# The first megabyte of keys in three strided transfers instead of one

## The chip, the core and the metric

The kernel runs on one core of a Trainium2 chip. The metric is the device time of one execution in microseconds. Three timed executions before the change gave 192.98, 193.03 and 193.13; their median is 193.03.

## The reference

Decode step of a gated mix of two branches: attention over a cached window and a small MLP. In short:

```
x: 8 x 1 x 448                    k_cache, v_cache: 8 x 8 x 4096 x 256 (bf16)
g = sigmoid((x * gate_w).sum(-1))
q = (x @ wq) as 16 heads of 256;  k, v = the last 1024 positions, each kv head used by 2 query heads
a = softmax(q k^T / 16) v, all heads side by side, @ wo
b = gelu(layernorm(x) @ w1 + b1) @ w2 + b2
out = g * a + (1 - g) * b
```

All inputs together that must be read are 77.67 MB, nearly all of it the 1024 cached positions of keys and values: 8 batches x 8 heads x 1024 x 256 x 2 bytes is 33.6 MB for each of the two.

## The kernel before

Everything large comes through one ring of four slots in SBUF (`ring`, `RING = 4`); a slot is 128 partitions x 32 KB, 4 MB. A list, `plan`, says in which order slots are filled: keys of batch 0, the weights wq, then for each further batch its keys and the values of the batch before it, then w1, the last values, and wo. `pump()` issues the loads of the next entries as long as fewer than four slots are in use, and `done()` frees one when its reader has been issued. All these loads are issued from one queue, SP (SyncE). Two small inputs, x and gate_w, are loaded from the ACT queue (L177, L182).

The keys of one batch are 8 heads x 1024 positions x 256. Partition p of a slot holds 32 consecutive positions: p = 4 s + a, where a is the head within a group of four heads and s (0 to 31) the block of 32 positions. One half of a slot is heads 0 to 3, the other heads 4 to 7. `kv_loader` makes one transfer for each half (16 KB in each partition, 2 MB), or more where `cuts` asks for it: for batch 0 it is `(2, 2)`, four transfers of 1 MB, each with 128 rows of 8 KB:

```
nc.sync.dma_start(
    t[:, i * HS + k * n : i * HS + (k + 1) * n],
    v[:, :, k * n : (k + 1) * n],
)
```

The source `v` has the dimensions s, a and (position in the block, head dimension); the destination `t` is taken over all 128 partitions.

Transfers are numbered round robin over eight completion semaphores in the order in which they are issued, those from ACT among them. So from the ninth on, each issue first waits until the transfer eight places before it has landed. Loads that refill a slot wait for its readers, too. SP's instructions run in order, so an issue that waits holds back all later ones.

The compute side, per batch: the keys are turned so that the head dimension lies on partitions. The first block of a batch goes by a 32 x 32 transpose on DVE (L334) and copies on POOL (L342), the other fifteen by TensorE transposes into PSUM (L364) and copies on ACT (L370) or DVE (L372). Then come scores (L431), maximum (L444), exponential (L448), the turning of the weights (L455 to L485), and the product with the values (L502). At the end TensorE multiplies by w2 and wo (L636, L647), the result is copied (L658) and stored (L659).

At the start nothing computes before keys or weights are there: L334 and L364 wait for the first MB of keys of batch 0, the query matmuls (L383, L395) for wq.

Of the kernel before, what the change touches and what calls it, by code (L numbers as in the profile page):

```python
# [17 lines left out]
def kernel(  # L18
# [15 lines left out]
    nc = tc.nc  # L34
# [11 lines left out]
    QD = 4  # L46
# [20 lines left out]
    HS = NCK * Dh  # L67
    SLOT = NG * HS
    RING = 4
    TAIL = 8  # L70
    LATE = 1
    qscale = float(Dh) ** -0.5

    xf = A_x.rearrange("b s d -> (b s) d")
# [30 lines left out]
    def add(key, loader):  # L105
        index[key] = len(plan)
        plan.append(loader)
# [1 line left out]
    def slot(*key):  # L109
        return slots[index[key]]  # L110

    def kv_loader(src, b, cuts=(1, 1), inner=False):
        pieces = [
            (i, k, cuts[i])
            for i in range(NG)
            for k in range(cuts[i])
        ]
        if inner:
            pieces.sort(key=lambda x: x[1])

        def load(t):
            for i, k, m in pieces:
                v = src[b, i * QD : (i + 1) * QD, kv_base:Sk, :].rearrange(
                    "a (s c) d -> s a (c d)", c=NCK
                )
                n = HS // m
                nc.sync.dma_start(
                    t[:, i * HS + k * n : i * HS + (k + 1) * n],
                    v[:, :, k * n : (k + 1) * n],
                )  # L130

        return load

    def rows_loader(pieces):
        def load(t):
            o = 0
            for ap in pieces:
                n = ap.shape[-1]
                nc.sync.dma_start(t[:, o : o + n], ap)
                o += n  # L140

        return load
# [11 lines left out]
    def last_values(t):  # L154
        kv_loader(A_v_cache, NB - 1, (2, 2), True)(t)
        nc.sync.dma_start(slot("w12")[:, OW2 : OW2 + FB * D], w2_v)

    add(("k", 0), kv_loader(A_k_cache, 0, (2, 2)))
    add(("wq",), rows_loader(wq_r + [wq_t]))
    for b in range(1, NB):  # L160
        add(("k", b), kv_loader(A_k_cache, b))
        add(("v", b - 1), kv_loader(A_v_cache, b - 1))
    add(("w12",), rows_loader([w1_m, w1_t]))
    add(("v", NB - 1), last_values)
    cuts = [(q, 0, J8) for q in range(NQW - 2)] + [
        (NQW - 2, 0, 4),
        (NQW - 2, 4, 8),
        (NQW - 1, 0, 2),
        (NQW - 1, 2, 5),
        (NQW - 1, 5, 7),  # L170
        (NQW - 1, 7, 8),
    ]
# [439 lines left out]
    b = NB - 1  # L612
# [30 lines left out]
    nc.vector.tensor_tensor(accs[:], A1[:], b2s[:], op=ALU.add)  # L643
    narrow.insert(TAIL - LATE, (pick[:], accs[:]))
    for i, (lhsT, rhs) in enumerate(narrow):
# [44 lines left out]
```

## Time and profile before

| | |
|---|---|
| median of 3 runs | 193.03 us (192.98 to 193.13) |
| the profiled execution, its own time | 193.1 us |
| its span, first to last instruction | 191.3 us |
| read from HBM | 77.67 MB, 406 GB/s over the span |
| busy: PE, DVE, ACT, POOL | 121.7, 108.5, 92.5, 55.6 us |
| first issue of keys on SP | at 0.73 us |
| first MB of keys landed | at 5.85 us |
| last weights landed, last PE group begins | at 186.32 and 186.36 us |

Times of events are counted from the start of the span. An engine's busy time doesn't include its waits. A transfer is issued by an instruction on a queue (SPq, ACTq), whose time is the time of issuing; the data are moved by 16 DMA engines, each taking whole rows as packets, and "landed" is when the waiting instruction could see the completion. The trace has every packet's start, size and duration, but not which of the 16 engines moved it.

### The profile page before, as it was taken

To read this page: it belongs to the slowest core of one execution; us is meant where nothing else is said; L and a number is where in the kernel's file an instruction comes from. 1 tells how busy PE (TensorE), PEld (TensorE's weight loads), DVE (VectorE), ACT (ScalarE), POOL (GpSimd) and SP (SyncE) were. 2 spreads that over 40 slices of the span, in tenths; PEclk is the share of its full clock that TensorE was granted. 3 is DMA by queue.
4 is the path that set the end of the run, shared out by engine and by line. 5 is a ranking of instruction groups with operands and counts; after the bars stand their busy time and mean duration, and the time that the engine had idled before them with its cause. 6 is when DMAs were issued, how large, how long until landed. Compare 5 with 4: busy or idle time off the path is not lost.

```text
span 191.3 us, 2889 instructions
## 1 busy us (share of the span) xinstructions
PE 121.7 (64%) x1100; PEld 78.9 (41%) x1100; DVE 108.5 (57%) x247; ACT 92.5 (48%) x104; POOL 55.6 (29%) x143
## 2 busy tenths in 40 slices
PE   0777609778775387737787677558944885073553
PEld 0656205564661186316642553156514762010111
DVE  4273783844889558705871587028722895846310
ACT  2398600994892259525862595229822892000000
POOL 8570000760760067005800480039002910000000
PEclk9997885999999969997996999859998899966555
DMA  5999999999999999999999999999999999999980
GB/s 190 432 423 426 445 423 418 414 438 432 421 430 415 432 432 425 433 428 414 425 435 432 435 411 425 432 421 433 428 421 428 425 432 406 420 422 428 409 334 4
DMA packets 7417, 77.86 MB, mean 407 GB/s; under 512 B 862, under 2 KB 1388, under 8 KB 2156
## 3 DMA queue, kind: packets, MB, share of 16 engines
q1 hardware_dynamic: 7370, 77.67, 96.5%
q8 instruction: 8, 0.13, 0.3%
q14 instruction: 5, 0.04, 0.1%
q10 hardware_dynamic: 34, 0.01, 0.0%
HBM read 77.67 MB, written 0.01 MB: 406 GB/s over the span
## 4 chain that ended last, share of the span: by engine, by line
DMA 75%; PE 10%; DVE 7%; ACT 4%; issue 1%; ACTq 0%; DVEq 0%
DMA slot<-in_A_k_cache_dram 45%; DMA slot<-in_A_v_cache_dram 14%; DMA slot<-in_A_wq_dram 8%; DMA slot<-in_A_wo_dram 7%; PE ktp L364 6%; ACT kt L370 3%; DVE kt L372 2%; PE S_ps L431 2%; DVE qw L423 1%; PE A L647 1%; DVE EZ L466 1%; DVE qt L408 1%; DVE nmx L444 1%; DVE EB L455 1%; DVE sc L464 1%
## 5 line engine op out<-in xcount | busy, mean ns | idle before, releaser
L370 ACT COPY kt<-ktp 128x1024 bf16<-128x1024 bf16 x80 | 76.7, 1020 | 37.7 <-PE ktp L364 37.4
L364 PE MATMUL ktp<-ident_f,slot 128*128 128x128 f32 x480 | 72.8, 307 | 29.7 <-DMA slot<-in_A_k_cache_dram 20.1
L364 PEld LDWEIGHTS ktp<-ident_f,slot 128*128 128x128 f32 x480 | 61.1, 158 | 48.4 <-issue 22.4
L342 POOL COPY kt<-B 32x128 f32<-32x128 f32 x128 | 51.4, 402 | 97.8 <-DVE B L334 92.8
L372 DVE COPY kt<-ktp 128x1024 bf16<-128x1024 bf16 x40 | 27.5, 687 | 17.0 <-PE ktp L364 16.8
L502 PE MATMUL PO<-slot,ET 128*16 128x512 bf16 x256 | 18.8, 441 | 17.6 <-DMA slot<-in_A_v_cache_dram 17.6
L334 DVE STREAM_TRANSPOSE B<-slot 128x512 f32<-128x512 f32 x8 | 5.7, 712 | 30.9 <-DMA slot<-in_A_k_cache_dram 30.8
L448 ACT ACTIVATE E<-S_ps,nmx 128x1024 f32<-128x1024 f32 x8 | 8.9, 1115 | 28.8 <-DVE nmx L444 28.8
L431 PE MATMUL S_ps<-kt,qw 128*4 128x512 bf16 x256 | 17.9, 419 | 5.4 <-DVE qw L423 5.4
L502 PEld LDWEIGHTS <-ET 128*16 128x16 bf16 x256 | 6.9, 96 | 28.5 <-DMA slot<-in_A_v_cache_dram 13.5
L444 DVE TENSOR_REDUCE nmx<-S_ps 128x1 f32<-128x1024 f32 x8 | 9.8, 1222 | 9.9 <-PE S_ps L431 9.9
L431 PEld LDWEIGHTS <-qw 128*4 128x4 bf16 x256 | 6.7, 85 | 13.5 <-DVE qw L423 6.2
L455 DVE STREAM_TRANSPOSE EB<-E 128x1056 f32<-128x1056 f32 x8 | 10.2, 1271 | 1.3 <-ACT E L448 1.3
L528 DVE TENSOR_TENSOR oP<-Y 32x32 bf16<-32x32 f32 x32 | 9.4, 295 | 1.1
L658 ACT CAST res<-A 8x224 bf16<-8x224 f32 x1 | 0.3, 337 | 15.8 <-PE A L647 15.8
L485 DVE TENSOR_TENSOR ET<-sm,mask 128x512 bf16<-128x512 f32 x8 | 5.5, 692 | 2.2 <-PE sm L477 2.1
L515 DVE STREAM_TRANSPOSE T<-PO 128x512 f32<-128x512 f32 x8 | 5.7, 709 | 1.0 <-PE PO L502 0.9
L570 ACT ACTIVATE zb<-za 128x448 f32<-128x448 f32 x1 | 0.6, 576 | 10.7 <-DVE za L569 10.7
L477 PE MATMUL sm<-EZ,perm 128*128 128x128 bf16 x8 | 1.7, 216 | 6.3 <-DVE EZ L466 6.3
L636 PE MATMUL A<-slot,oP 128*8 128x448 bf16 x24 | 2.9, 549 | 2.5 <-DMA slot<-in_A_wo_dram 2.5
L643 DVE TENSOR_TENSOR accs<-A,b2s 128x448 f32<-128x448 f32 x1 | 0.6, 625 | 6.6 <-PE A L636 6.6
L520 DVE TENSOR_TENSOR Y<-T 64x64 f32<-64x64 f32 x16 | 4.0, 248 | 0.6
(91 smaller groups left out, 59.6 us busy)
## 6 DMA issues: line engine op xcount, KB each, us to landing
slot<-in_A_k_cache_dram SPq DMA_DIRECT2D x14, 2048.0 KB, 28.9
slot<-in_A_v_cache_dram SPq DMA_DIRECT2D x14, 2048.0 KB, 30.8
slot<-in_A_k_cache_dram SPq DMA_DIRECT2D x4, 1024.0 KB, 10.6
slot<-in_A_v_cache_dram SPq DMA_DIRECT2D x4, 1024.0 KB, 24.8
slot<-in_A_wq_dram SPq DMA_DIRECT2D x3, 1024.0 KB, 13.3
slot<-in_A_wo_dram SPq DMA_DIRECT2D x2, 896.0 KB
slot<-in_B_w_dram SPq DMA_DIRECT2D x1, 1568.0 KB, 22.4
slot<-in_B_w_dram SPq DMA_DIRECT2D x1, 1344.0 KB
```

What stands on the lines that cost most here:

```text
L334: nc.vector.transpose(B[:].rearrange("p c w s a -> p (c w s a)"), kn[:, c0 * P : (c0 + CB) * P],)
L342: nc.gpsimd.tensor_copy(words[BL * w : BL * (w + 1), :, c0 : c0 + CB, g * S8 : (g + 1) * S8, 0], B[BL * g : BL * (g + 1), :, w].rearrange( ...
L364: nc.tensor.transpose(words[:, c, :, 0], kn[:, o : o + P], ident_f[:])
L370: nc.scalar.copy(dst, src)
L372: nc.vector.tensor_copy(dst, src)
L431: nc.tensor.matmul(S_ps[BL * t : BL * t + UR, n * QN : (n + 1) * QN], lhsT=qw[:, j, b, t, rep * u : rep * u + UR], rhs=KT[u][:, t, n * CQ ...
L444: nc.vector.reduce_max(nmx[:], S_ps[:], axis=AXIS.X, negate=True)
L448: nc.scalar.activation(E[:, 0:W], S_ps[:], ACT.Exp, bias=soft.pop(b)[:], scale=1.0, accum_out=E[:, W : W + 1],)
L455: nc.vector.transpose(EB[:].rearrange("p c r -> p (c r)"), E[:])
L502: nc.tensor.matmul(PO[BL * t : BL * t + Hq], lhsT=ET[:, c].rearrange("p u a r -> p (u a r)"), rhs=vn[:, c], start=(c < QD), stop=(c >= NCK ...
L515: nc.vector.transpose(T[:], PO[:].rearrange("p u (e j) -> p u j e", j=J8))
L528: nc.vector.tensor_tensor(oP[BL * i : BL * (i + 1), :, :, b], Yv[0:BL, :, :, i], Yv[BL : 2 * BL, :, :, i], op=ALU.add,)
```

## The change

Of the four 1 MB transfers of batch 0's keys, the first is split by partitions into three: partitions 0, 4, 8, ... (head 0, 32 rows), partitions 2, 6, 10, ... (head 2, 32 rows), and the odd partitions (heads 1 and 3, 64 rows). Rows are still 8 KB each, and each lands where it did. The other three transfers of that slot and all other loads stay as they were. The two more transfers stand on the SP queue ahead of everything that followed the first one, and take two more places in the round of semaphores.

```
+    FIRST = ((0, QD), (2, QD), (1, 2))
...
-    def kv_loader(src, b, cuts=(1, 1), inner=False):
+    def kv_loader(src, b, cuts=(1, 1), inner=False, first=((0, 1),)):
...
                 n = HS // m
-                nc.sync.dma_start(
-                    t[:, i * HS + k * n : i * HS + (k + 1) * n],
-                    v[:, :, k * n : (k + 1) * n],
-                )
+                for a, step in first if (i, k) == (0, 0) else ((0, 1),):
+                    nc.sync.dma_start(
+                        t[a::step, i * HS + k * n : i * HS + (k + 1) * n],
+                        v[:, a::step, k * n : (k + 1) * n],
+                    )
...
-    add(("k", 0), kv_loader(A_k_cache, 0, (2, 2)))
+    add(("k", 0), kv_loader(A_k_cache, 0, (2, 2), first=FIRST))
```

`QD` is 4. For all other pieces the loop runs once, over all partitions, as before.

## The prediction

> **What bounds the kernel now.** I read the page from the top, first for what is never idle.
>
> ```profile
> PE   0777609778775387737787677558944885073553
> ...
> DMA  5999999999999999999999999999999999999980
> ...
> HBM read 77.67 MB, written 0.01 MB: 406 GB/s over the span
> ...
> DMA 75%; PE 10%; DVE 7%; ACT 4%; issue 1%; ACTq 0%; DVEq 0%
> ```
>
> PE, the busiest engine, has holes in nearly every slice. The DMA row has only three that are not full, the first and the last two. Three quarters of the chain that ended last are transfers. Next, the table by stages (columns: stretch and its us, five engines, PEclk, DMA share, GB/s) shows how full "9" is, and how the stream begins.
>
> ```profile
> 2.13:2.53 0.40, 0.00 (x0) 0.00 (x0) 0.34 (x2) 0.40 (x1) 0.40 (x2) 1.00 1.89 328
> 2.53:2.93 0.40, 0.00 (x0) 0.00 (x0) 0.36 (x2) 0.38 (x1) 0.40 (x2) 1.00 0.00 0
> 2.93:3.33 0.40, 0.00 (x0) 0.00 (x0) 0.14 (x2) 0.00 (x0) 0.40 (x3) 1.00 1.26 532
> ...
> 6.00:60.00 54.00, 40.16 (x338) 27.96 (x338) 35.44 (x92) 35.01 (x39) 19.27 (x48) 0.91 1.01 427
> 60.00:120.00 60.00, 39.69 (x375) 27.39 (x376) 36.27 (x76) 32.63 (x37) 19.29 (x48) 0.91 1.01 427
> 120.00:180.00 60.00, 36.19 (x343) 21.75 (x343) 33.79 (x73) 23.22 (x27) 12.85 (x32) 0.83 1.01 424
> ```
>
> A packet counts in the stretch in which it starts. All 16 DMA engines start their first key row (8 KB) between 2.13 and 2.53; nothing starts in the next 0.4 us; the second rows start from 2.93. From there the engines run without a break to 186.3 us. The same rate holds whichever engine computes, so the time is: start of the stream + 77.67 MB at the DMA engines' rate + the tail. A DMA engine that starts earlier by some time ends the kernel earlier by that time, if its share and its rate stay. The tail, in the chain of waits:
>
> ```profile
> 172.03 14.29 DMA slot<-in_A_wo_dram
> 186.32 0.04 issue
> 186.36 2.11 PE A L647 x16
> 188.47 0.37 DVE res L658
> ```
>
> It follows the last weights and moves with them. So all depends on the first three microseconds, in the timeline and in the DMA view of 1.4 to 2.6 us (40 slices of 30 ns):
>
> ```profile
> 0.73 0.59 ACTq L177 DMA_DIRECT2D x_sb<-in_A_x_dram  x1
> 0.73 2.59 SPq L127 DMA_DIRECT2D slot<-in_A_k_cache_dram  x4
> 5.88 0.71 DVE L334 STREAM_TRANSPOSE B<-slot 128x512 f32<-128x512 f32 x1 [2.81 <-DMA slot<-in_A_k_cache_dram]
> ...
> DMA  0000000001670000000000000999999999000900
> GB/s 0 0 0 0 0 0 0 0 0 60 120 60 0 0 0 0 0 0 0 0 0 0 0 0 0 819 273 819 273 273 819 273 273 273 0 0 0 273 0 0
> ```
>
> Two transfers are issued at the same 0.73 us: x_sb, 8 rows, from ACT, and the first MB of keys, 128 rows, from SP. The rows of x_sb begin at 1.68 to 1.74 (packet starts in the trace; slices 10 to 12 above), those of the keys at 2.17 to 2.52 (slices 26 to 38), mean 2.28. So 0.95 us after the issue with 8 rows, and 1.44 us with 128.
>
> **The change, part by part.**
>
> *Earlier start of the first row.* The transfer at the head of the queue shrinks from 128 rows to 32. A straight line through the two rows above gives 0.95 + 24/120 x 0.49 = 1.05 us from issue to first packet, and the spread over the engines shrinks from 0.35 us toward the 0.05 of x_sb: 0.11. Mean start 0.73 + 1.05 + 0.06 = 1.84 instead of 2.28: gain 0.44. Lower bound 0: the two rows differ in the issuing engine and in the size of a row, too, and if the delay hangs on those nothing moves. I take the line, as the only pair that the trace has.
>
> *First row's duration.* The first key rows take 0.64 to 0.95 us (mean 0.76 over the 16 packets), all later ones of 8 KB 0.31 (median of the packets), so 0.45 us more; 6 of 8 rows of x_sb took 0.04 to 0.05, the bare time of 896 bytes. If the excess comes with the 128 rows, a line gives back 0.3 of it; if it belongs to the first access to key rows, nothing. The new first rows are key rows of 8 KB, nearest to the latter: gain 0.1, bounds 0 and 0.3.
>
> *Two more transfers on SP.* The issues of L127 take 0.54 to 0.66 us whether 8 or 16 KB a row, and L187 with only 2 rows (also at a partition step) 0.53 and 0.59, so rows do not matter to SP and I price each new one like these, 0.64 with its gap (the first four start 0.63 to 0.72 apart). All later issues on SP move back by 2 x 0.64 = 1.3 us: the second MB is issued at 2.7 instead of 1.45, the four wq transfers from 4.6 instead of 3.37. What covers it is the queue. Piece one starts at 1.84 and gives each engine 2 rows: 0.66 + 0.31, drained at 2.8. Piece two, issued at 1.4, is ready at 2.4 to 2.5, and lasts 0.62 to 3.4. Piece three, issued at 2.1, with 64 rows (line: 1.18) is ready at 3.3, lasts 1.24 to 4.7; the second MB, issued at 2.7, is ready at 4.15. Each is there before the one ahead is drained, with 0.1 to 0.5 us to spare, so it costs nothing. Without that cover (first row at its bare 0.31) piece two and three come 0.1 to 0.2 late, bound 0.2. The waits of SP's later issues on older transfers shift by two places: the wq loads now wait for x_sb, for the first two key pieces and for gate_w's row, all long landed by 4.6 to 6; k(1) waits for the third piece, issued then at about 6.3 against 6.24. From k(1)'s second half on, each waits for the same transfer as before. With 3 MB and more queued (7 us) none empties the stream.
>
> *Two more boundaries on each DMA engine.* A transfer ends on each engine with a 4-byte packet of 9 ns, and the next row starts some 10 ns later; rows just behind it take 0.31 to 0.32. So 2 x 0.02 us, and I take 0.05.
>
> *Rows and bytes* stay: 128 rows of 8 KB, the same addresses, 8 rows per engine if each piece is dealt out evenly (2, 2 and 4). The consumers (L334, L364) now wait for three transfers, of which the last lands earlier than the one does now (5.85). What was idle before them stays idle, and no engine's order changes.
>
> Sum: -0.44 - 0.10 + 0 + 0.05 = -0.49 us. The profiled execution took 193.1 (span 191.3 and 1.8 around it), so 192.6; the median is 0.07 lower: **192.55**. With all bounds: -0.44 - 0.3 + 0.05 = -0.7 to +0.25 (no gain, 0.2 late, 0.05).
>
> [...]
>
> **The rivals.**
>
> *A. The start does not move enough.* The 1.44 us come from the key rows or from SP's slower issue (0.66 against 0.59 on ACT), not from the number of rows. For: the pieces stay strided in SBUF, and L187 shows that SP needs no less for few rows. Against: between end of issue and first packet lie 0.37 us for x_sb and 0.78 for the keys, and that difference is the larger part. Time 192.7 to 193.3, most likely 192.9.
>
> *B. Slower: two DMA engines meet at one place of SBUF.* The trace shows 0.31 us per 8 KB row only for transfers of all 128 partitions. In a piece of every fourth or second partition the dealing of rows to engines is another, and where two engines write into the same part of SBUF at once they would halve each other's rate. All 8 rows of the first MB: 8 x 0.31 = +2.5, less 0.5: 195.0; in half of the rows: +1.24 - 0.49, 193.8. It decides from where the mean row of the first MB takes over 0.31 + 0.88/8 = 0.42 us (0.49 to eat the gain, 0.39 to be seen). For: no row of the trace excludes it. Against: each piece reaches across all of SBUF, and engines out of step would pass each other. [...]
>
> *C. Slower: uneven dealing.* If the small pieces of 32 rows fell on 8 engines, those would have 4 rows more each: +1.24, 193.8. Against it: the 8 rows of x_sb went to 8 engines, one each, with 8 closing packets.
>
> **How the numbers follow.** 0.2% is 0.39 us, about what a measurement of this kernel can tell from no change. Forecast (192.2 to 192.64): 0.50, since the sum needs only 0.39 of its 0.49 and the second term's bound lies above. A: 0.20, the part of the lower bounds that stays within 0.39. B: 0.22, half of it near 193.8 and half up to 195. C: 0.08. So faster 0.50, same 0.20, slower 0.30. The range reaches from all gains at their bounds with a little over for the boundary price (192.2) over A and the half-rate cases near 193.8 to 194.2, and leaves out the full case of B and of C, about 0.15, and little below. The likeliest case alone: 192.2 to 192.64.
>
> **What would show it.** In the changed profile: first key packets at 1.8 to 1.9 us instead of 2.17; no pause in packet starts after 2.9; rows of 0.31 us in the first MB; the third piece landed and L334 begun at about 5.4 instead of 5.88; the last PE group at 185.9 instead of 186.36; DMA share 1.01 in between; the end 5.0 us after. Wrong: a first packet at 2.1 or later (A); packets of 0.4 to 0.6 us before 5 us (B); engines that begin the second MB more than a row apart (C); or a stretch without packets between the pieces, which would mean that SP feeds too slowly.

## The result, and the profile after

The changed kernel took 195.24 us (median of 6 runs, 194.47 to 195.57) against 193.01 for the kernel before (6 runs, 192.98 to 193.13): ratio 1.0108, 95% interval 1.009 to 1.0126. It is slower by 2.2 us, outside the range that was forecast. The profiled execution took 194.9, with a span of 193.1 against 191.3.

Lines of the page of the changed kernel, those that answer to the ones shown of before:

```profile
DMA  5999999999999999999999999999999999999970
...
HBM read 77.67 MB, written 0.01 MB: 402 GB/s over the span
...
DMA 71%; PE 11%; ACT 6%; DVE 6%; SPq 3%; issue 2%; ACTq 0%
```

The bytes are the same and the DMA row looks the same. New is SPq with 3% in the chain that ended last: issuing on SP has become part of it. The table by stages of the changed kernel (columns as in the prediction; a packet counts in the stretch in which it starts) shows where the time went:

```profile
2.20:4.00 1.80, 0.00 (x0) 0.00 (x0) 0.77 (x4) 0.70 (x1) 1.80 (x6) 1.00 0.99 337
4.00:5.00 1.00, 0.00 (x0) 0.00 (x0) 0.00 (x0) 0.00 (x0) 0.82 (x2) 1.00 0.86 287
5.00:6.50 1.50, 0.00 (x0) 0.00 (x0) 0.00 (x0) 0.00 (x0) 0.00 (x0) 1.00 0.99 306
6.50:8.00 1.50, 1.22 (x6) 1.25 (x7) 0.71 (x1) 0.10 (x1) 0.41 (x2) 1.00 0.84 317
8.00:60.00 52.00, 37.42 (x322) 25.71 (x324) 33.23 (x87) 34.77 (x39) 18.75 (x47) 0.93 1.01 425
60.00:180.00 120.00, 75.77 (x724) 49.87 (x712) 70.10 (x151) 55.61 (x64) 32.00 (x80) 0.86 1.01 425
```

The kernel before in the first stretch and in the three that differ:

```profile
2.20:4.00 1.80, 0.00 (x0) 0.00 (x0) 0.77 (x4) 0.71 (x1) 1.80 (x6) 1.00 0.98 333
4.00:5.00 1.00, 0.00 (x0) 0.00 (x0) 0.00 (x0) 0.00 (x0) 0.83 (x2) 1.00 0.96 401
5.00:6.50 1.50, 0.51 (x3) 0.54 (x4) 0.62 (x1) 0.00 (x0) 0.00 (x0) 1.00 1.01 421
6.50:8.00 1.50, 1.50 (x9) 1.50 (x8) 0.13 (x2) 0.89 (x1) 1.22 (x4) 1.00 1.02 431
```

The last column is the one to read. Up to 4 us both move the same, then the changed kernel moves 287, 306 and 317 GB/s for 4 us where the kernel before moves 401 to 431, and from 8 us on there is no difference worth the name. The packet records say it in time: the first 0.5 MB are through at 3.78 us against 3.89 before, so 0.1 earlier; 1 MB at 5.49 against 5.08, 2 MB at 8.63 against 7.47, 3 MB at 11.10 against 9.82, and 70 MB at 168.70 against 167.46. About 1.25 us are lost by 11 us and stay lost. Between 2.2 and 11 us the 16 engines stood idle for 0.57 us each on average (0.04 before), and their rows took 1.23 us more than the usual 0.31 us a row (0.49 before). The two increases, 0.53 and 0.74, make 1.27 us. So the longer rows are the larger part.

The first stretches of the changed kernel answer to the three of the prediction: there is no pause of 0.4 us any more, since in this execution the first rows took less time (0.48 us on average, 0.76 before), but the third stretch has 351 GB/s instead of 532.

```profile
2.13:2.53 0.40, 0.00 (x0) 0.00 (x0) 0.34 (x2) 0.40 (x1) 0.40 (x2) 1.00 0.91 246
2.53:2.93 0.40, 0.00 (x0) 0.00 (x0) 0.36 (x2) 0.37 (x1) 0.40 (x2) 1.00 0.87 328
2.93:3.33 0.40, 0.00 (x0) 0.00 (x0) 0.14 (x2) 0.00 (x0) 0.40 (x3) 1.00 1.03 351
```

The start itself, in the DMA view of 1.4 to 2.6 us of the changed kernel and in its timeline:

```profile
DMA  0000000005020000000000000009999090000099
GB/s 0 0 0 0 0 0 0 0 0 179 1 60 0 0 0 0 0 0 0 0 0 0 0 0 0 0 0 546 819 819 273 0 819 0 0 0 0 0 546 546
...
0.73 3.77 SPq L129 DMA_DIRECT2D slot<-in_A_k_cache_dram  x6
4.55 3.45 SPq L141 DMA_DIRECT2D slot<-in_A_wq_dram  x4
...
6.77 0.71 DVE L336 STREAM_TRANSPOSE B<-slot 128x512 f32<-128x512 f32 x1 [3.70 <-DMA slot<-in_A_k_cache_dram]
```

Key rows begin in slice 28 (2.22 us), later than the slice 26 of before. The third piece has landed at 6.77, 0.9 us later than the whole MB did. SP issues the six key transfers 0.63 us apart, as priced, but the first two wq transfers take 0.98 and 1.17 us to issue (0.63 and 0.43 before). The tail, in the chain of waits of the changed kernel, has its old length:

```profile
173.81 14.25 DMA slot<-in_A_wo_dram
188.06 0.04 issue
188.10 2.11 PE A L649 x16
190.21 0.37 DVE res L660
```

It comes 1.74 us later. That is more than the 1.25 us of the stream, in part because the DMA engines now end further apart: the 16 closing packets of the last transfer lie at 187.36 to 188.44 (mean 187.75), before at 186.00 to 186.73 (mean 186.32). Mean +1.43, last +1.71: the tail, +1.74, goes with the last. (The profiled execution was one of the quicker ones of the changed kernel, 0.3 us below its median.)

### The profile page after: what moved, and what is told of

Same layout as the page of the kernel before. It is cut to its first block, busy times and chain, and to the rows that moved or that the text cites. A ratio compares the mean times of both kernels' runs of the same rounds, so it can differ in the third digit from the quotient of the medians.

```text
span 193.1 us, 2893 instructions
## 1 busy us (share of the span) xinstructions
PE 121.6 (63%) x1100; PEld 79.0 (41%) x1100; DVE 107.7 (56%) x247; ACT 92.1 (48%) x104; POOL 55.3 (29%) x143
## 4 chain that ended last, share of the span: by engine, by line
DMA 71%; PE 11%; ACT 6%; DVE 6%; SPq 3%; issue 2%; ACTq 0%
DMA slot<-in_A_k_cache_dram 42%; DMA slot<-in_A_v_cache_dram 13%; DMA slot<-in_A_wq_dram 9%; DMA slot<-in_A_wo_dram 7%; PE ktp L366 7%; ACT kt L372 5%; PE S_ps L433 2%; SPq L129 2%; SPq L141 1%; DVE kt L374 1%; DVE qw L425 1%; PE A L649 1%; DVE qt L410 1%; DVE nmx L446 1%; DVE EZ L468 1%
## 5 line engine op out<-in xcount | busy, mean ns | idle before, releaser
L366 PE MATMUL ktp<-ident_f,slot 128*128 128x128 f32 x480 | 73.7, 310 | 31.2 <-DMA slot<-in_A_k_cache_dram 22.3
L366 PEld LDWEIGHTS ktp<-ident_f,slot 128*128 128x128 f32 x480 | 61.8, 160 | 49.8 <-issue 25.4
L504 PE MATMUL PO<-slot,ET 128*16 128x512 bf16 x256 | 18.0, 427 | 16.5 <-DMA slot<-in_A_v_cache_dram 16.5
L504 PEld LDWEIGHTS <-ET 128*16 128x16 bf16 x256 | 6.3, 94 | 27.6 <-DMA slot<-in_A_v_cache_dram 18.8
```

The source lines that it names most:

```text
L366: nc.tensor.transpose(words[:, c, :, 0], kn[:, o : o + P], ident_f[:])
L504: nc.tensor.matmul(PO[BL * t : BL * t + Hq], lhsT=ET[:, c].rearrange("p u a r -> p (u a r)"), rhs=vn[:, c], start=(c < QD), stop=(c >= NCK ...
```

## Experiments

**Partition steps, or the number of transfers.** Rival B (here theory M) had the right size, so the first four runs part it from a queue that is fed too slowly (theory Q).

```diff
 e1_columns: the first MB by columns
+    for lo, hi in ((0, 0.25), (0.25, 0.5), (0.5, 1)):   # of the 8 KB of a row
+        nc.sync.dma_start(t[:, i * HS + c0 : i * HS + c1], v[:, :, c0:c1])
```

> The first MB again in three transfers of 256, 256 and 512 KB, but cut by columns: each has all 128 partitions, with rows of 2, 2 and 4 KB. Number, bytes and order on SP are those of the changed kernel. Theory M (in a piece with a partition step, DMA engines meet at one place of SBUF and slow each other): no meeting here, so 193.0 or a little below (192.6 to 193.2), packets of 2 KB at about 0.08 us. Theory Q (the queue is fed too slowly when transfers at its head are small; the partitions do not matter): about 195, as changed, with DMA engines idle between 4 and 7 us.

195.31 us, ratio 1.0116 (1.0099 to 1.0133): the loss of the change, without a partition step.

```diff
 e2_ranges: the first MB by ranges of partitions
+    for s0, s1 in ((0, 8), (8, 16), (16, 32)):
+        nc.sync.dma_start(t[4 * s0 : 4 * s1, ...], v[s0:s1, :, ...])
```

> The first MB in three transfers of 32, 32 and 64 rows as in the changed kernel, but of neighbouring partitions (0-31, 32-63, 64-127) instead of every fourth or second. Theory M: the meeting depends on how rows are dealt; ranges reach fewer places in SBUF at a time, so as slow as the change or slower (195 to 196.5). Theory Q: the same as the change, 195.2 within 0.4.

195.95 us, ratio 1.0154 (1.0136 to 1.0173), 0.7 more than the change. The table by stages of e1, then of e2:

```profile
4.00:5.00 1.00, 0.22 (x1) 0.25 (x2) 0.50 (x1) 0.00 (x0) 1.00 (x3) 1.00 0.87 260
5.00:6.50 1.50, 0.86 (x4) 0.46 (x3) 0.00 (x0) 0.60 (x1) 1.35 (x4) 1.00 1.10 300
```
```profile
6.50:8.00 1.50, 0.00 (x0) 0.00 (x0) 0.00 (x0) 0.00 (x0) 0.00 (x0) 1.00 0.90 191
```

e1 has the same hole as the change (the stretches in which it moves less than the kernel before), at the same time. Its rows are longer than usual as well: up to 11 us they take 1.29 us more for each engine than rows of their size in the median (0.084 us for 2 KB, 0.159 for 4 KB), as against 1.23 in the change. So rows get longer without partition steps, too.

e2 loses time in two other ways, and the runs don't part them. The first lies at the start:

```profile
2.20:4.00 1.80, 0.00 (x0) 0.00 (x0) 0.77 (x4) 0.69 (x1) 1.80 (x6) 1.00 0.44 146
```

Each of its two pieces of 32 rows ends with 8 closing packets (4.08 to 4.30 and 5.31 to 5.53 us), and up to 4.1 us only 8 rows are under way at a time. So 8 engines took 4 rows each: the uneven dealing of rival C. In the change the pieces of 32 rows end with 16 closing packets each (2.99 to 3.39 and 3.70 to 4.01 us). The second way is that from 6.5 to 8 us e2 moves 191 GB/s with the engines busy (share 0.90), and 29 of the 35 rows of 8 KB that start there take 0.59 to 0.66 us, twice 0.31. By the closing packets 8 engines are then still in the third piece, partitions 64 to 127 (they close it at 7.37 to 8.55), while the others, through with it at 6.31 to 6.40, have gone on to the second MB. The doubled rows fit rival B's supposition of two engines that meet in SBUF, but no view shows which engine writes where, so that cause is not shown. The change has no such stretch of doubled rows (of the 58 that start from 6.5 to 8 us, 42 take 0.31 to 0.32 us, the longest 0.59); its loss is another.

```diff
 e3_midstream: the same split, in the middle of the stream
-    add(("k", 0), kv_loader(A_k_cache, 0, (2, 2), first=FIRST))
+    add(("k", 0), kv_loader(A_k_cache, 0, (2, 2)))
...
+    add(("k", b), kv_loader(A_k_cache, b, first=FIRST if b == 4 else ((0, 1),)))
```

> The first MB whole, as before; the same three-way split by partition steps is put on the first half of batch 4's keys, 2 MB with rows of 16 KB, in the middle of the stream, where over 6 MB are queued ahead. Theory M: twice the bytes meet, so at least the loss of the change, 195 to 197, and packets of 16 KB well over 0.61 us there. Theory Q: the queue is full, so nothing is lost: 193.0 within 0.2.

193.14 us, ratio 1.0006 (0.9997 to 1.0016): free, with twice the bytes. In its stage from 60 to 180 us, where the split lies (issued at 62.5), the rate is that of the kernel before:

```profile
60.00:180.00 120.00, 76.71 (x718) 50.17 (x719) 69.74 (x148) 55.70 (x63) 32.13 (x80) 0.84 1.01 425
```

A loss of 1.25 us in these 120 us would have lowered it by 1%, to some 421. Theory M falls for this change; the loss needs the head of the queue.

```diff
 e4_tiny_between: behind the whole first MB, on SP
+    for e in range(2):
+        nc.sync.dma_start(spare[BL * e : BL * (e + 3) : 2 * BL, :], b1[2 * e : 2 * e + 2, :])
```

> The first MB whole, as before, followed on SP by two added transfers of 2 rows x 896 bytes into a tile that nothing reads: SP issues the second MB 1.2 us later, and all later waits shift by two places, as in the change. Theory M: 193.0 within 0.2. Theory Q in the form that the later issues and shifted waits starve the queue: 194 to 195.5; in the form that only the small pieces starve it: 193.0 to 193.4.

193.12 us, ratio 1.0001 (0.9991 to 1.001). The second MB is issued at 2.66 us as in the change, and all waits are shifted as in the change, at no cost. So SP's later issues alone are not it.

**Size, order and place of the pieces.** Theory S: a short transfer is drained before the next is ready. Theory C: a fixed cost of each added transfer.

```diff
 f1_halves        FIRST = ((0, 2), (1, 2))
 f2_large_first   FIRST = ((1, 2), (0, QD), (2, QD))
 f3_second_mb     if (i, k) == (0, 1)          # the second MB split, not the first
 f4_two_queues    eng = nc.sync if a == 0 else nc.scalar
```

> The first MB in two transfers of 64 rows (even and odd partitions): only one transfer more than before. Theory S (a transfer's rows can move only some 2.2 to 3 us after its issue, so a short transfer at the head of the queue is drained before the next is ready): 4 rows per DMA engine last 1.7 us with the slow first one, the second half is issued at 1.4 and ready at about 3.6, the first is drained at about 3.9: loss at most 0.3, 192.8 to 193.4. Theory C (each added transfer at the start costs a fixed 1.1 us, whatever its size and whatever lies ahead): 194.1.

194.47 us, ratio 1.0076 (1.0061 to 1.0091): nearer to theory C. In its stages the hole lies behind the second half:

```profile
4.00:5.00 1.00, 0.00 (x0) 0.00 (x0) 0.00 (x0) 0.00 (x0) 0.82 (x2) 1.00 0.91 319
5.00:6.50 1.50, 0.00 (x0) 0.00 (x0) 0.00 (x0) 0.00 (x0) 0.00 (x0) 1.00 0.60 208
6.50:8.00 1.50, 1.24 (x6) 1.27 (x7) 0.71 (x1) 0.12 (x1) 0.46 (x2) 1.00 1.03 393
```

By the packet records 8 engines close the second half at 5.10 to 5.17 us, and until 6.0 us only 8 rows are under way at a time; each of these follows straight on another. The idle engines take their next rows from 6.04 on. Those rows belong to the second MB, which SP had issued at 2.06: half of the engines began it 4.0 us or more after its issue, having stood idle for 0.9 or more. The prediction's price for it, 1.44 us from issue to first packet, does not hold here.

> The same three pieces as in the change in another order: the 64 rows of the odd partitions first, then 32 and 32. Theory S: the first piece covers 1.2 us more; the two small ones still drain in 0.6 us each, so a part of the loss stays: 193.0 to 194.3. Theory C: 195.2.

193.81 us, ratio 1.0043 (1.0028 to 1.0058).

> The first MB whole, the second MB split in 32, 32 and 64 rows by the same partition steps: same number and size of transfers as in the change, one place later in the queue, with the 2.5 us of a whole MB ahead. Theory S: 193.0 to 193.4. Theory C: 195.2.

193.67 us, ratio 1.0033 (1.0019 to 1.0047). The same three transfers cost 2.2 us at the very head, 0.8 when the largest goes first and 0.6 behind a whole MB: theory C's fixed cost falls with these two, S's course is right, its sizes are not (f1, f3).

> The three pieces of the change, but the second and third are issued from the ACT queue, ahead of x_sb there, so that the second MB is issued from SP at 1.4 us instead of 2.6. Theory S: there is more work ready early, 192.8 to 194. Theory C: 195.2.

194.55 us, ratio 1.0074 (1.0049 to 1.0099), 193.75 to 194.99 in single runs. In the profiled run, the fastest, the stream lost only 0.12 us but the engines ended 0.95 us apart (0.73 before). In that run the stream was helped and the end was not; for the slower runs this is inconclusive.

**What a transfer costs at the head.** Theory D: handing a transfer over to the engines lags once data move, whatever its bytes. Theory L: only bytes count. Theory P: the delay of the first packet goes by the form of the first transfer.

```diff
 g1_tiny_all: as e4, but 128 rows of 64 bytes each
+    nc.sync.dma_start(spare[:, 32 * e : 32 * (e + 1)], wq_m[:, 32 * e : 32 * (e + 1)])
 g2_column_halves: two transfers of 128 rows x 4 KB instead of the first MB
 g3_two_mb_first: cuts (1, 2) instead of (2, 2) for batch 0
 g4_wq_first: ahead of batch 0's keys
+    nc.sync.dma_start(w[:, 0:HD], wq_r[0])
```

> As e4_tiny_between, but each of the two added transfers has 128 rows of 64 bytes, so that all 16 DMA engines take part in it (8 packets and a closing one each). Theory D (handing a transfer over to the 16 engines takes 1.2 to 1.7 us each once data move, one after the other in the order of issue, whatever its bytes; f1_halves gives this figure: its third transfer comes at 5.9 us): the first is there at 2.2, these two by 3.7 and 5.2, the second MB at 6.4 to 6.9 instead of 5.1: 194 to 195. Theory L (only the bytes ahead of a transfer count, the added ones are drained while the first MB runs): 193.0 to 193.3, as e4_tiny_between.

193.74 us, ratio 1.0033 (1.0021 to 1.0046). Two transfers with 16 KB in all cost 0.66 us, less than theory D's 1 to 2 and clearly more than theory L's nothing. Against e4 all engines take part, and there are 256 rows instead of 4; the runs don't part these two. Their own packets take 0.17 us of each engine (256 packets, 11 ns in the median); much of the rest is the hole again, in g1's stages (its profiled execution, 194.27, was the slowest of six):

```profile
5.00:6.50 1.50, 0.39 (x2) 0.42 (x3) 0.50 (x1) 0.00 (x0) 0.00 (x0) 1.00 0.78 235
```

> The first MB in two transfers of 512 KB as in f1_halves, but cut by columns: 128 rows of 4 KB each instead of 64 rows of 8 KB. Theory D, cost per transfer: as f1_halves, 194.5 within 0.4. If the cost goes by rows: twice the rows, so 195 or more. If the partition step were behind f1's loss after all: 193.0.

194.49 us, ratio 1.008 (1.0065 to 1.0095): the same as f1, with twice the rows and without a step. The cost goes by transfers, not by rows or by partition steps.

> The other direction: the first half of batch 0's keys whole, 2 MB with rows of 16 KB, so that the head of the queue covers 5 us instead of 2.5. Theories D and S: no loss to begin with, so nothing or a little to gain: 192.9 to 193.1.

192.88 us, ratio 0.9991 (0.9982 to 1.0001): all ten runs between 192.82 and 193.01, a small gain that the interval does not quite part from none.

> The first MB of wq (128 rows of 8 KB, plain rows on neighbouring partitions, issued in 0.33 to 0.63 us) is put ahead of batch 0's keys, which stay four transfers of 1 MB. Theory P (the first packet's delay depends on the form of the transfer, not on its rows: 0.95 us for x_sb's plain rows, 1.42 to 1.52 for keys with 32, 64 and 128 rows): first packet about 1.0 us after the issue, the stream 0.3 to 0.45 earlier: 192.55 to 192.75. Otherwise (the queue or the size of a row sets the delay): 193.0.

192.81 us, ratio 0.9995 (0.9982 to 1.0007); nine runs lie between 192.76 and 192.92 and one at 193.97. The first packets come where theory P puts them, in the DMA view of 1.4 to 2.6 us of g4 from slice 12 on (547 GB/s is two rows of 8 KB started in 30 ns):

```profile
DMA  0000000002999990909999009000099009909090
GB/s 0 0 0 0 0 0 0 0 0 90 120 547 303 273 819 0 546 0 273 273 546 273 0 0 273 0 0 0 0 273 273 0 0 273 273 0 273 0 273 0
```

By the packet records the first one starts 1.02 us after the issue, where the key loads of all these runs took 1.35 to 1.52 with 32, 64 or 128 rows (e2's range of 32: 1.81). That is 0.42 us earlier than before, and the stream (70 MB) came out 0.23 us earlier, half of it.

**Where the cost comes from.**

```diff
 h2_late_whole / h3_late_split: the kernel before / the changed one, held back
+    nc.gpsimd.memset(t[:, 0:HS // 2], 0.0)      # ahead of the first key load
 h4_plain_pieces: as g4, wq's first MB by columns
+    for o, n in ((0, HD // 4), (HD // 4, HD // 4), (HD // 2, HD // 2)):
+        nc.sync.dma_start(w[:, o : o + n], wq_r[0][:, o : o + n])
 h1_long_head: as g4, and batch 0's keys in two transfers of 2 MB
```

> The kernel before, with its first load held back by some 4 us: POOL first zeroes the part of the slot that the first MB then fills. To be compared with h3_late_split. Both theories: the kernel before plus the delay, about 197.

196.58 us, 3.5 us above the kernel before.

> The changed kernel, held back in the same way. Theory D: the loss belongs to the queue's own start, so h3 is slower than h2 by 1.5 to 2.5 us, with DMA engines idle some 2 to 4.5 us after the first row. Theory T (something that every execution does between 4 and 6.5 us after its start holds up the handing over of transfers): the pieces come later than that, so h3 equals h2 within 0.4.

198.39 us, 1.81 above h2. The first issue of both is at 4.27 us, so all stretches lie 3.54 us later. h2, then h3:

```profile
7.55:8.55 1.00, 0.00 (x0) 0.00 (x0) 0.00 (x0) 0.00 (x0) 0.72 (x2) 1.00 0.94 393
8.55:10.05 1.50, 0.61 (x3) 0.64 (x4) 0.71 (x1) 0.00 (x0) 0.00 (x0) 1.00 1.04 431
```
```profile
7.55:8.55 1.00, 0.00 (x0) 0.00 (x0) 0.00 (x0) 0.00 (x0) 0.72 (x2) 1.00 0.94 303
8.55:10.05 1.50, 0.00 (x0) 0.00 (x0) 0.00 (x0) 0.00 (x0) 0.00 (x0) 1.00 0.78 300
```

The hole moves with the queue's start, so nothing that the execution does at a fixed time makes it (theory T falls). x_sb, loaded long before in these two, has no part in it either.

> As g4_wq_first, but wq's first MB at the head is cut by columns into 256, 256 and 512 KB: three transfers of plain rows (128 rows of 2, 2 and 4 KB). If the cost hangs on every transfer that all DMA engines share: slower than g4 by 1 to 2.4 us, 193.9 to 195.2. If it hangs on the strided form of the key loads (0.53 to 0.66 us on SP against 0.33 to 0.45): within 0.4 of g4, 192.8 to 193.2.

195.22 us, ratio 1.0109 (1.0085 to 1.0132), 2.4 above g4: plain rows lose as much as strided ones. The rows are longer here too, by 1.25 us for each engine (g2: 1.24).

> The version that the runs point to: wq's first MB, in plain rows, at the head, and batch 0's keys in two transfers of 2 MB behind it. Theory D (a cost per transfer at the head, whatever its bytes) with theory P (plain rows start earlier): the gains of g4_wq_first and g3_two_mb_first in part together, 192.6 to 192.8. If the two gains are the same one: 192.8 to 192.9.

192.67 us, ratio 0.998 (0.997 to 0.9989), ten runs between 192.63 and 192.84: faster than both kernels. Its tail, in the chain of waits, begins 0.29 us earlier than that of the kernel before:

```profile
186.07 2.12 PE A L661 x16
```

The last two runs try whether enough work ahead covers everything. The edits: wq's first 3 MB as one transfer at the head of h1 (i1), and g1's two small transfers behind 2 MB instead of 1 (i2).

> One step further than h1_long_head: the first three megabytes of wq in one transfer (128 rows of 24 KB) at the head, then batch 0's keys in two of 2 MB: two transfers fewer, 7 us of work in the first one. Theory D: the head is covered in h1 already, so little is left to gain: 192.55 to 192.75. If each transfer costs something even where it is covered: 192.4.

193.25 us, ratio 1.0006 (0.9997 to 1.0016): no gain. The mean closing packet of the last transfer is earlier than before (185.96 against 186.32), the last one hardly (186.58 against 186.73).

> g1_tiny_all (two transfers of 128 rows x 64 bytes) with the first half of batch 0's keys whole ahead of them: 5 us of work instead of 2.5. Theory D: the same two transfers are handed over while the first runs and cost nothing: 192.85 to 193.1. If they cost what they cost in g1 whatever lies ahead: 193.5 to 193.8.

193.72 us, ratio 1.0029 (1.0019 to 1.0038), as g1 and against theory D. The hole is gone in i2's profile (of the slowest of its ten runs, 194.01): its stream loses 0.2 us around the two transfers, little more than their own packets. But its engines end 1.37 us apart (186.21 to 187.58; 0.73 before), and the time goes with the last one: it lies 0.85 us later than before, and this run took 0.95 more than the median of the kernel before (193.06).

## Why the prediction was wrong

*Right:* the DMA engines bind from end to end, so what the stream loses at its start, the end loses (1.28 us at 3 MB, 1.24 at 70 MB); the tail keeps its length (2.11 us on PE and 0.37 on DVE in both); SP issues the new transfers 0.63 us apart, with 32 rows as with 64 and 128; two more boundaries in a full queue cost next to nothing (e3: 0.1 us, within its interval of none).

*The failed step* is "Two more transfers on SP ... it costs nothing", with its bound of 0.2. It took the delay from issue to first packet at the head of the queue, 1.05 to 1.44 us by its line, as the price of every transfer. Behind the first, once data move, that price doesn't hold: in f1 half of the engines began a transfer only 4.0 us or more after its issue. In the change the queue of short transfers ran dry between them, and the rows around these gaps took longer (0.53 and 0.74 us). The term was mis-sized: 0 in the sum, 1.25 us of stream in the profiled run, and 0.3 to 0.5 us more because the engines then end further apart, a term that the sum did not have. Together they make nearly all of the 1.74 us by which the tail came later there; the median run lost 0.3 us more and has no profile. The prediction's sign for it was there ("a stretch without packets between the pieces"), but its reason, that SP feeds too slowly, was not: e4 delays SP as much and loses nothing.

*The gain of 0.44 us* was not there either. A straight line through 8 rows and 128 rows took the rows for the cause; with 32 rows the first packet came 1.49 us after the issue. g4, h1, h4 and i1, with 128 plain rows, needed 1.02 to 1.06, so the number of rows is not behind it. The form of the transfer may be, or its source: the plain rows are all of wq, the others of the key cache. Rival A was right that it is not the rows. *The 0.10 us of the first row* was a difference between executions: 0.76 us on average in the profiled run of before, 0.39, 0.49 and 0.41 in e3, e4 and f3 with the same first transfer.

*Rival B* named 195.0 and the time came near it, for another reason. Its sign, packets of 0.4 to 0.6 us before 5 us, is in the trace; but e1 and h4 lose as much as the change, and g2 as much as f1, with all 128 partitions in each piece and rows lengthened by as much as in the change (1.24 to 1.29 us). A stretch of rows at half rate, as it describes them, was seen in e2 only (0.59 to 0.66 us), and that two engines meeting in SBUF cause it is not shown there either. *Rival C's* sign is there as well: the engines close the third piece between 5.07 and 6.34 us, more than a row apart. But each of the three pieces ends with 16 closing packets, so all engines took part in each; the uneven dealing itself is seen in e2, with 8.

One transfer over all 128 partitions was the better choice at the head of the queue, where splitting cost 1.4 us for two pieces (f1, g2) and 2.2 for three; in the middle of the stream (e3) it made no difference. The number of transfers decides here, not the partitions that each reaches: with all 128 in each of three pieces e1 lost 2.3 us, and h4 2.4 against g4.

*Open:* what lags between the issue on SP and the engines, and why the rows around a gap take longer; no view shows it, nor which engine moved a packet. Why small all-engine transfers leave the engines apart even behind 2 MB (i2), and why i1's earlier stream doesn't become an earlier end, is open too.

## What to carry to other kernels

Where transfers bind, begin the queue with few and large ones: splitting the first megabyte to start sooner cost 2.2 us, and the same split in a full queue cost nothing. The first packet came sooner with plain rows of wq at the head, not with a smaller transfer (1.02 us after the issue in g4, 1.49 in the change, 1.44 before). Together with two key transfers of 2 MB instead of four of 1 MB that made the kernel 0.2% faster (h1). Read the spread of the engines' last packets as well as the mean rate: in the change the end came 1.74 us later, the last closing packet 1.71, the mean one 1.43.

## What the hardware showed that was not expected

- Half of the DMA engines stood idle for 0.9 us or more and began a transfer 4.0 us or more after its issue (f1), while the first one of all had moved 1.5 us after its issue.
- Two transfers of 128 rows of 64 bytes behind the first MB cost 0.66 us (g1); two of 2 rows of 896 bytes cost nothing (e4).
- First packets came 1.02 to 1.06 us after the issue with plain rows, and 1.35 to 1.52 us after it with the key loads, from 32 to 128 rows (1.81 in e2).
- Pieces of 32 neighbouring partitions ran on 8 engines (e2: 8 closing packets each, 146 GB/s), pieces of 32 at a step of 4 on all 16.
- Where 8 engines were in a piece of partitions 64 to 127 and 8 in the next transfer, rows of 8 KB took 0.59 to 0.66 us instead of 0.31 (e2); with steps of 4 and 2 there was no such stretch.
